# A half tile of the contraction as two 64-row matmuls on two PSUM banks, with one pool of three PSUM tiles for the product and the transform

## The chip, the cores and the metric

One Trainium2 chip, one of its cores. The metric is the device time of one execution in microseconds (us). TensorE (PE) multiplies matrices from SBUF into PSUM, loading one operand as weights (PEld) and streaming the other; ScalarE (ACT), VectorE (DVE) and GpSimd (POOL) do the elementwise work; SyncE (SP), ACT and POOL issue DMAs.

## The reference

The input `A_q` (2048 x 448) is normalised over its last axis, and three things are added: the input, a gated long convolution (A), and a two-layer perceptron with Mish (B).

```
def _A_ref(q, k, v, shift_k, ssm_k, ssm_D):          # S = 2048, D = 448
    k_shift = sum of 4 taps of k along S, each times shift_k[:, tap]
    kv = k_shift * v
    y = irfft(rfft(kv, 2 S) * rfft(ssm_k, 2 S))[:S] + kv * ssm_D
    return q * y
def _B_ref(x, w1, b1, w2):                           # F = 1792
    h = x @ w1 + b1
    act = h * tanh(softplus(h))                      # Mish
    return act @ w2
x = A_q
xn = _layernorm(x)
return x + _A_ref(xn, A_k, A_v, A_shift_k, A_ssm_k, A_ssm_D) + _B_ref(xn, B_w1, B_b1, B_w2)
```

## The kernel before

**The perceptron.** The 2048 rows go in 8 chunks of 256 (`CH`), the 1792 inner features in 14 tiles of 128, taken in pairs: 8 x 7 = 56 pairs (chunk c, pair p). Operands are float32, and the matmuls take a faster form that is rounded, so each operand is split into a rounded high part and the rest: `w1h` and `w1l`, `XH` and `XL`. A product is then high x high, low x high and high x low.

The contraction of the first product has 448 rows: three tiles of 128 and a half tile of 64. The half tile is packed: the input carries its 64 weight rows twice, and `tail` repeats the last 64 columns of the normalised x, so that tile 3 of x has the same 64 rows in both halves. `w1_lo` (L341) replaces rows 64 to 127 of tile 3 of `w1h` by the low part of the weights. One full matmul with tile 3 thus gives high plus low weights in one go.

`g1_mm` (L433) does one pair: for each of two inner tiles n, into its half of one PSUM bank, 3 high-high, 3 high-low and 3 low-high matmuls, and two with tile 3, one for `XH` (`th`) and one for `XL` (`tl`): 22 matmuls of 128 x 128 by 256 columns. `mish` (L449) reads the bank with two activations on ACT, then splits the result (`split`, L72: a copy on ACT and a subtraction on DVE). `g2_mm` (L461) multiplies by w2, two pairs later (`G2_LAG`).

**The transform.** The long convolution is done as matrix products in float32 with small tiles of the array (32 or 64 rows by 32 or 64 columns), in bursts: `f1_mm` (L117, two PSUM tiles, read by `f1_fold` on ACT and DVE), `f2_mm` (L201, one tile each, copied out by ACT), `i1_mm` (L243, two tiles, copied out by ACT) and `i2_mm` (L300, one tile, read by `gate` on DVE). Between the stages the data goes through DRAM.

**The x tiles.** For the next chunk, `ln_T` (L420) transposes the normalised x on TensorE into a PSUM tile, once in the odd slot of the last pair but one and once in the even slot of the last pair; ACT makes `XH` of it (L418) and DVE `XL` (L416).

**PSUM.** It has 8 banks. `g1p` holds two tiles of one bank, for `g1_mm` and `ln_T` in turn; `g2p` two of one bank, for `g2_mm`; `pcp` two of two banks, for the bursts. A pool hands out its tiles in turn, and the first write to a tile waits until what was in it has been read.

**The order** is written out by hand. Each pair has two slots. `mlp_slot` does `g1_mm(i)` in the even one, and in the odd one `mish(i)` and `g2_mm(i - 2)`. `plan` holds work to be put ahead of a slot's perceptron part and `plan2` work behind it; the dictionaries at the top and the loops from L519 on fill them. Each engine takes its instructions in this order. `drip` is a list of small DVE steps (the statistics of the next chunk), which `dv` lets in between others, and which `ln_T` empties.

Of the kernel before, what the change touches and what calls it, by code (L numbers as in the profile page):

```python
# [7 lines left out]
F32 = mybir.dt.float32  # L8
# [3 lines left out]
PSUM = bass.MemoryType.PSUM  # L12
# [6 lines left out]
CH = 256  # L19
# [18 lines left out]
def tile_kernel(ctx: ExitStack, tc, q, k, v, sk, hT, sD, w1, b1, w2, c_f1, c_g, c_gi, c_i2, out):  # L38
    nc = tc.nc
    V = nc.vector  # L40

    def pool(name, bufs=1, stack=ctx, **kw):
        return stack.enter_context(tc.tile_pool(name=name, bufs=bufs, **kw))
# [1 line left out]
    cp = pool("consts")  # L45
    wp = pool("weights")
    mp = pool("mlp")
    g1p = pool("ps_g1", 2, space=PSUM)
    g2p = pool("ps_g2", 2, space=PSUM)
    pcp = pool("ps_c", 2, space=PSUM)  # L50
    dp = pool("scratch", space=DRAM)


# [13 lines left out]
    w1h = wp.tile([128, 4, F], F32R, name="w1h")  # L67
# [4 lines left out]
    def split(h, l, raw):  # L72
        nc.scalar.copy(h, raw)  # L73
        V.tensor_sub(l, raw, h)  # L74

    def pc():
        return pcp.tile([128, 2, 512], F32, name="pc")
# [4 lines left out]
    def dv(n=1):  # L82
        for _ in range(n):
            if drip:
                drip.pop(0)()
# [246 lines left out]
    RW = {}  # L332
# [8 lines left out]
    def w1_lo(p, a=0, b=256, engs=(V, V)):  # L341
        fs, rw = slice(256 * p + a, 256 * p + b), RW["1", p][:, :, a:b]
        if engs[0]:
            engs[0].tensor_sub(w1l[:, :, fs], rw[:, 0:3], w1h[:, 0:3, fs])
        if engs[1]:
            engs[1].tensor_sub(w1h[64:128, 3, fs], rw[64:128, 3], w1h[64:128, 3, fs])

    def w1_split(p):
        w1_hi(p)
        w1_lo(p)  # L350
# [11 lines left out]
    def ln_load(c, eng=None):  # L362
        Q[c] = mp.tile([128, 2, D], F32, name="qt", tag="qt", bufs=3)
        if c:
            nc.sync.dma_start(Q[c], q[:, 2 * c:2 * c + 2])
        else:
            for jj in range(2):
                nc.sync.dma_start(Q[c][:, jj], q[:, jj])
# [30 lines left out]
    def ln_stats(c):  # L399
        stats, aggr, eps, power, norm, tail = ln_parts(c)  # L400
        drip.extend([lambda: stats(0), lambda: stats(1), lambda: aggr(0), lambda: aggr(1), lambda: eps(0, 2),
                     lambda: [f(*a) for f, *a in ((power, 0, 2), (norm, 0), (norm, 1), (tail, 0, 2))]])

    def transposes(c, jj, p):
        for kt in range(4):
            nc.tensor.transpose(p[:, 128 * kt:128 * kt + 128], XN[c][:, jj, 128 * kt:128 * kt + 128], ident)  # L406

    def x_tiles(c):
        XS[c] = (mp.tile([128, 4, CH], F32R, name="XH", tag="XH", bufs=2),
                 mp.tile([128, 4, CH], F32R, name="XL", tag="XL", bufs=2))  # L410

    def x_split(c, jj, p, lo):
        x = p.rearrange("p (a b) -> p a b", a=4)
        h, l = (t[:, :, 128 * jj:128 * jj + 128] for t in XS[c])
        if lo:
            V.tensor_sub(l, x, h)  # L416
        else:
            nc.scalar.copy(h, x)  # L418

    def ln_T(c, jj):  # L420
        if jj == 0:
            dv(len(drip))
            x_tiles(c)
        p = g1p.tile([128, 2, CH], F32, name="pg1").rearrange("p a b -> p (a b)")
        transposes(c, jj, p)
        for lo in range(2):
            x_split(c, jj, p, lo)
# [5 lines left out]
    def g1_mm(i):  # L433
        c, p = pairs[i]
        XH, XL = XS[c]
        ps = g1p.tile([128, 2, CH], F32, name="pg1")
        for n in range(2):
            f = 2 * p + n
            fs = slice(128 * f, 128 * f + 128)
            mm = []  # L440
            hh, hl, lh = ([(w[:, kt, fs], x[:, kt]) for kt in range(3)] for w, x in ((w1h, XH), (w1h, XL), (w1l, XH)))
            th, tl = ((w1h[:, 3, fs], x[:, 3]) for x in (XH, XL))

            mm = hh + hl + lh + [th, tl] if i == 0 and n else hh + lh + [th] + hl + [tl]
            for n_, (l, r) in enumerate(mm):
                nc.tensor.matmul(ps[:, n], l, r, start=n_ == 0, stop=n_ == len(mm) - 1)  # L446
        P1[i] = ps

    def mish(i):  # L449
        p = pairs[i][1]  # L450
        ps = P1.pop(i)
        a = mp.tile([128, 2, CH], F32, name="a", bufs=2)
        for n in range(2):
            nc.scalar.activation(a[:, n], ps[:, n], AF.Mish, bias=b1t[:, 2 * p + n:2 * p + n + 1])  # L454
        ah = mp.tile([128, 2, CH], F32R, name="ach", bufs=3)
        al = mp.tile([128, 2, CH], F32R, name="acl", bufs=3)
        split(ah, al, a)
        dv()
        AHL[i] = ah, al

    def g2_mm(i, jjs=(0, 1)):  # L461
        c, p = pairs[i]
        ah, al = AHL[i]
        for n in range(2):
            f = 2 * p + n
            for jj in jjs:
                if f == 0:
                    P2[c, jj] = g2p.tile([128, 512], F32, name="pg2")
                ps = P2[c, jj][:, :D]
                cs = slice(128 * jj, 128 * jj + 128)  # L470
                nc.tensor.matmul(ps, ah[:, n, cs], w2h[:, f], start=f == 0, stop=False)  # L471
                nc.tensor.matmul(ps, ah[:, n, cs], w2l[:, f], start=False, stop=False)  # L472
                nc.tensor.matmul(ps, al[:, n, cs], w2h[:, f], start=False, stop=f == NF - 1)  # L473

    def g2_evac(c, jjs=(0, 1)):
        x = Q[c]
        for jj in jjs:
            V.tensor_add(x[:, jj], P2.pop((c, jj))[:, :D], x[:, jj])  # L478
            dv()
            if late(c):  # L480
                nc.sync.dma_start(out[:, 2 * c + jj], x[:, jj])
        if not late(c):
            nc.sync.dma_start(out[:, 2 * c:2 * c + 2], x)

    def mlp_slot(s):
        i, half = divmod(s, 2)
        n = len(pairs)
        j = i - G2_LAG
        if half == 0:
            if i < n:  # L490
                c, p = pairs[i]
                if c + 1 < NCHUNK:
                    if p == 0:
                        ln_load(c + 1)
                    if p == (2 if c else 3):
                        ln_stats(c + 1)
                    if c == 0:
                        dv(len(drip))
                    if p == NP - 1:
                        ln_T(c + 1, 1)  # L500
                g1_mm(i)
        else:
            if i < n:
                c, p = pairs[i]
                if p == NP - 2 and c + 1 < NCHUNK:
                    ln_T(c + 1, 0)
                mish(i)
            if 0 <= j < n - 1:
                g2_mm(j)
            elif j == n - 1:  # L510
                for jj in range(2):
                    g2_mm(j, (jj,))
                    g2_evac(pairs[j][0], (jj,))
# [94 lines left out]
    ps = [g2p.tile([128, 512], F32, name="pg2") for _ in range(2)]  # L608
    x_tiles(0)
    for jj in range(2):  # L610
        norm(jj)
        tail(jj, jj + 1)
        transposes(0, jj, ps[jj])
        x_split(0, jj, ps[jj], 0)
    w1_lo(0, 0, 128)
    w1_hi(0, 128, 256)
    w1_lo(0, 128, 256, (nc.gpsimd, None))
    for jj in range(2):
        x_split(0, jj, ps[jj], 1)
# [3 lines left out]
    for s in range(nslots):  # L623
        j = s // 2 - G2_LAG - 1
        if s % 2 == 0 and j >= 0 and pairs[j][1] == NP - 1:
            g2_evac(pairs[j][0])
        for fn, args in plan.pop(s, ()):
            fn(*args)
        mlp_slot(s)
        for fn, args in plan2.pop(s, ()):  # L630
            fn(*args)
# [63 lines left out]
```

## Time and profile before

| | |
|---|---|
| median of 3 runs | 375.84 us (372.77 to 376.81) |
| profiled execution, first to last instruction (its span) | 370.5 us; its whole time is not among the numbers |
| PE busy | 361.2 us, 98%, 3128 matmul instructions |
| PEld (weight loads) busy | 292.2 us, 79% |
| DVE, ACT, POOL busy | 261.4 us (71%), 165.9 us (45%), 71.2 us (19%) |
| mean granted clock of TensorE | 1.000 |

The profile follows one execution. A row of the timeline reads: start, length, engine, line of the kernel, operation, tile written <- tiles read, rows * columns of the array, shapes, count; in brackets the engine's idle time before it and what ended it. Rows with a count are several instructions in one. Matmuls overlap in the records, so their spacing, and not their length, tells what one costs. A row of the groups reads: busy us, mean ns of one | idle time before.

### The profile page before, as it was taken

What the parts mean: (1) busy time and instruction counts of PE and PEld (TensorE: products, weight loads), DVE (VectorE), ACT (ScalarE), POOL (GpSimd) and SP (SyncE); (2) the same over time, 40 slices, a digit from 0 to 9 for tenths busy, and PEclk for the clock granted to TensorE, in tenths of its full rate; (3) what the DMA queues carried; (4) which work ended last, traced back from release to release, by engine and by line L of the source; (5) the groups of instructions that cost most, each with busy time, mean ns of one, the idle gap of its engine ahead of it and who ended that gap; (6) DMA issues with size and microseconds to landing.
All of it is one profiled execution on the core that took longest, in us unless ns stands there. A gap on an engine that the chain in (4) does not pass through costs nothing.

```text
span 370.5 us, 7467 instructions
## 1 busy us (share of the span) xinstructions
PE 361.2 (98%) x3128; PEld 292.2 (79%) x3128; DVE 261.4 (71%) x358; ACT 165.9 (45%) x277; POOL 71.2 (19%) x59
## 2 busy tenths in 40 slices
PE   8999999999998999999999999999999999999995
PEld 2889888888887988988886666666666879889885
DVE  4899748999968987996435647654474842997751
ACT  2785642343423333343353556555475533235450
POOL 2107002722070223520014000060000005102020
PEclk9999999999999999999999999999999999999999
DMA  8999968757596428504876498988494475949655
GB/s 307 319 308 355 382 233 233 215 159 239 145 294 184 104 58 262 179 25 99 264 235 216 135 282 239 272 271 237 134 328 110 105 239 207 407 195 293 102 69 129
DMA packets 31442, 79.35 MB, mean 214 GB/s; under 512 B 2865, under 2 KB 18098, under 8 KB 31410
## 3 DMA queue, kind: packets, MB, share of 16 engines
q1 hardware_dynamic: 19826, 44.35, 35.4%
q10 hardware_dynamic: 9248, 22.61, 23.0%
q0 software_dynamic: 2336, 11.93, 11.3%
q8 instruction: 24, 0.39, 0.4%
q14 instruction: 8, 0.07, 0.0%
HBM read 50.44 MB, written 28.44 MB: 213 GB/s over the span
## 4 chain that ended last, share of the span: by engine, by line
PE 62%; DVE 4%; ACT 2%; ACTq 1%; issue 1%; DVEq 0%
PE pg L446 24%; PE pg L471 8%; PE pg L473 8%; PE pg L472 8%; PE pc L207 7%; PE pc L250 3%; PE pc L307 2%; PE pc L124 1%; PE pg L406 1%; ACTq L261 1%; ACT a L454 1%; DVE x L171 1%; DVE yc L240 1%; DVE qt L478 0%; ACT XH L418 0%
## 5 line engine op out<-in xcount | busy, mean ns | idle before, releaser
L454 ACT ACTIVATE a<-pg,b1t 128x256 f32<-128x256 f32 x112 | 47.1, 472 | 101.4 <-PE pg L446 80.6
L446 PE MATMUL pg<-XH,w1h 128*128 128x256 f32 x448 | 91.2, 285 | 0.7 <-ACT XH L418 0.7
L446 PEld LDWEIGHTS pg<-XH,w1h 128*128 128x128 f32 x448 | 69.5, 188 | 18.1 <-issue 15.7
L471 PE MATMUL pg<-w2h,ach 128*128 128x448 f32 x224 | 83.0, 371 | 0.0
L472 PE MATMUL pg<-w2l,ach 128*128 128x448 f32 x224 | 81.4, 363 | 0.6 <-DVE w2l L74 0.6
L473 PE MATMUL pg<-w2h,acl 128*128 128x448 f32 x224 | 81.4, 363 | 0.0
L74 DVE TENSOR_TENSOR acl<-a,ach 128x512 fp32r<-128x512 f32 x56 | 38.8, 692 | 55.2 <-ACT ach L73 55.0
L446 PE MATMUL pg<-XL,w1h 128*128 128x256 f32 x448 | 69.6, 277 | 0.0
L446 PEld LDWEIGHTS pg<-XL,w1h 128*128 128x128 f32 x448 | 59.4, 188 | 0.1
L446 PE MATMUL pg<-XH,w1l 128*128 128x256 f32 x336 | 56.9, 278 | 0.0
L471 PEld LDWEIGHTS pg<-w2h,ach 128*128 128x128 f32 x224 | 42.0, 187 | 11.6 <-issue 9.4
L446 PEld LDWEIGHTS pg<-XH,w1l 128*128 128x128 f32 x336 | 46.8, 188 | 0.1
L472 PEld LDWEIGHTS pg<-w2l,ach 128*128 128x128 f32 x224 | 42.1, 188 | 3.5 <-DVE w2l L74 1.1
L473 PEld LDWEIGHTS pg<-w2h,acl 128*128 128x128 f32 x224 | 42.1, 188 | 2.5
L387 POOL TENSOR_TENSOR rstd<-ve,mhalf 128x2 f32<-128x2 f32 (+1 forms) x9 | 8.5, 945 | 162.6 <-DVE ve L384 105.8
L73 ACT CAST ach<-a 128x512 fp32r<-128x512 f32 x56 | 34.7, 620 | 1.8
L154 POOL TENSOR_TENSOR x<-kr,skb 128x896 f32<-128x896 f32 x8 | 17.0, 2129 | 74.9 <-DVE x L153 54.1
L171 DVE TENSOR_TENSOR x<-x 128x896 f32<-128x896 f32 x24 | 26.6, 1107 | 5.1 <-POOL x L154 4.4
L391 POOL TENSOR_SCALAR xn<-qt,mv,rstd 128x448 f32<-128x448 f32 x12 | 26.7, 2231 | 0.6
L418 ACT CAST XH<-pg 128x512 fp32r<-128x512 f32 x16 | 9.4, 587 | 38.7 <-PE pg L406 35.5
L416 DVE TENSOR_TENSOR XL<-pg,XH 128x512 fp32r<-128x512 f32 x16 | 10.9, 687 | 15.5 <-ACT XH L418 15.3
L130 ACT COPY st<-pc 128x896 f32<-128x896 f32 x16 | 14.5, 908 | 14.7 <-PE pc L124 12.8
(71 smaller groups left out, 401.1 us busy)
## 6 DMA issues: line engine op xcount, KB each, us to landing
Dh<-st ACTq DMA_DIRECT2D x16, 448.0 KB, 6.0
Dkv<-st ACTq DMA_DIRECT2D x16, 448.0 KB, 5.1
ah<-Dh SPq DMA_DIRECT2D x8, 896.0 KB, 6.8
av<-Dkv SPq DMA_DIRECT2D x8, 896.0 KB, 5.9
E<-qe ACTq DMA_DIRECT2D x16, 448.0 KB, 5.4
e<-E POOLq DMA_DIRECT2D x8, 896.0 KB, 7.7
kr<-in_k_dram SPq DMA_DIRECT2D x10, 448.0 KB, 6.2
kr<-in_w_dram SPq DMA_DIRECT2D x7, 512.0 KB, 6.3
```

The costliest lines, as they stand in the source:

```text
L73: nc.scalar.copy(h, raw)
L74: V.tensor_sub(l, raw, h)
L130: nc.scalar.copy(st[:, 1], o)
L154: nc.gpsimd.tensor_mul(o, KR[g - u // 2], skb[:, u:u + 1].to_broadcast([128, 2, D]))
L171: V.tensor_add(KV[g], KV[g], o)
L207: nc.tensor.matmul(p[32 * t:32 * t + 32, r, :D], g[rs, t, c], a[rs, t], start=True, stop=True, tile_position=(64 * r, 32 * t))
L391: eng.tensor_scalar(xn[:, jj, :D], Q[c][:, jj], mv[:, j, 0:1], rstd[:, j:j + 1], op0=ALU.subtract, op1=ALU.mult)
L446: nc.tensor.matmul(ps[:, n], l, r, start=n_ == 0, stop=n_ == len(mm) - 1)
L454: nc.scalar.activation(a[:, n], ps[:, n], AF.Mish, bias=b1t[:, 2 * p + n:2 * p + n + 1])
L471: nc.tensor.matmul(ps, ah[:, n, cs], w2h[:, f], start=f == 0, stop=False)
L472: nc.tensor.matmul(ps, ah[:, n, cs], w2l[:, f], start=False, stop=False)
L473: nc.tensor.matmul(ps, al[:, n, cs], w2h[:, f], start=False, stop=f == NF - 1)
```

## The change

Four edits belong together.

1. In `g1_mm`, the matmul with tile 3 and `XL` goes for both inner tiles. In its place stand, at the end of the pair, two matmuls of 64 rows: the first with rows 0 to 63 for inner tile 0, the second with rows 64 to 127 for inner tile 1, each with high weights and low x. The product of low weights and low x, which the full matmul gave as well, is not made any more for these 64 rows.
2. So that the second finds high weights in rows 64 to 127, `w1_lo` puts the low part of the odd inner tiles into rows 0 to 63; it is now one subtraction for each 128 columns.
3. The two matmuls write to two banks, so `g1_mm` takes a tile of two banks. `g1p` is gone; the pool `pcp` has three tiles, in turn for `g1_mm`, `ln_T` and the transform's bursts.
4. In the odd slot of the last pair but one, `mish(i)` comes ahead of `ln_T(c + 1, 0)`.

```
-    g1p = pool("ps_g1", 2, space=PSUM)
     g2p = pool("ps_g2", 2, space=PSUM)
-    pcp = pool("ps_c", 2, space=PSUM)
+    pcp = pool("ps_c", 3, space=PSUM)
...
         if engs[1]:
-            engs[1].tensor_sub(w1h[64:128, 3, fs], rw[64:128, 3], w1h[64:128, 3, fs])
+            for n in range(a // 128, b // 128):
+                rs, fs = slice(64 - 64 * n, 128 - 64 * n), slice(256 * p + 128 * n, 256 * p + 128 * n + 128)
+                engs[1].tensor_sub(w1h[rs, 3, fs], RW["1", p][rs, 3, 128 * n:128 * n + 128], w1h[rs, 3, fs])
...
-        p = g1p.tile([128, 2, CH], F32, name="pg1").rearrange("p a b -> p (a b)")
+        p = pc()[:, 0]
...
-        ps = g1p.tile([128, 2, CH], F32, name="pg1")
+        ps = pc()[:, :, :CH]
...
-            th, tl = ((w1h[:, 3, fs], x[:, 3]) for x in (XH, XL))
-
-            mm = hh + hl + lh + [th, tl] if i == 0 and n else hh + lh + [th] + hl + [tl]
+            th = w1h[:, 3, fs], XH[:, 3]
+            mm = hh + hl + lh + [th] if i == 0 and n else hh + lh + [th] + hl
             for n_, (l, r) in enumerate(mm):
-                nc.tensor.matmul(ps[:, n], l, r, start=n_ == 0, stop=n_ == len(mm) - 1)
+                nc.tensor.matmul(ps[:, n], l, r, start=n_ == 0, stop=False)
+        for n in range(2):
+            rs, f = slice(64 * n, 64 * n + 64), 2 * p + n
+            nc.tensor.matmul(ps[:, n], w1h[rs, 3, 128 * f:128 * f + 128], XL[rs, 3], start=False, stop=True, tile_position=(64 * n, 0))
...
+                mish(i)
                 if p == NP - 2 and c + 1 < NCHUNK:
                     ln_T(c + 1, 0)
-                mish(i)
```

## The prediction

> **What bounds the kernel now.** I read the page first (busy times, chain), then the groups by line and shape, then TensorE's timeline stage by stage, then for each PSUM tile its first write against its last read.
>
> ```profile
> span 370.5 us, 7467 instructions
> PE 361.2 (98%) x3128; PEld 292.2 (79%) x3128; DVE 261.4 (71%) x358; ACT 165.9 (45%) x277; POOL 71.2 (19%) x59
> PE 62%; DVE 4%; ACT 2%; ACTq 1%; issue 1%; DVEq 0%
> ...
> L446 PE MATMUL pg<-XL,w1h 128*128 128x256 f32 x448 | 69.6, 277 | 0.0
> ...
> 137.66 2.51 PE pg L446 x22
> ```
>
> TensorE is busy 98% of the span and is most of the chain, so every microsecond added to its in-order stream, or that it waits, lengthens the run nearly one for one. The first product of one pair is 22 matmuls in 2.51 us (last row, from the chain), 0.114 us each. The two x-low half tiles are 2 of the 8 XL matmuls a pair (448 / 56).
>
> **The pair of half tiles.** The change removes two full matmuls, 2 x 0.114 = 0.23 us a pair, and adds two 64-row ones that could run side by side. No row shows 64 rows x 128 columns. The nearest are the transform's bursts, which also leave the full array for a row tiling:
>
> ```profile
> 102.58 0.23 PEld L124 LDWEIGHTS pc<-x,f1id 32*64 32x64 f32 x16 [0.31 <-issue]
> ...
> 183.24 0.62 PE L446 MATMUL pg<-XL,w1h 128*128 128x256 f32 x4
> 183.79 1.73 PE L207 MATMUL pc<-ah,g 64*32 64x448 f32 x32
> ...
> 184.19 1.33 PE L207 MATMUL pc<-ah,g 64*32 64x448 f32 x24
> ...
> 184.56 0.96 PE L207 MATMUL pc<-ah,g 64*32 64x448 f32 x16
> 185.45 0.47 PE L471 MATMUL pg<-w2h,ach 128*128 128x448 f32 x1
> 185.76 0.36 PE L472 MATMUL pg<-w2l,ach 128*128 128x448 f32 x1
> 185.97 0.37 PE L473 MATMUL pg<-w2h,acl 128*128 128x448 f32 x1
> ```
>
> Tiles do run side by side: 32 instructions go in four rounds of eight, and a round costs 0.37 (184.19 to 184.56). But each visit has a price outside its streams. Going in: four full matmuls from 183.24 should end at 183.24 + 4 x 0.114 = 183.70, yet the burst starts at 183.79: 0.09. Coming out: the last two rounds start at 184.56 and the next full matmul at 185.45, so 0.89 less 2 x 0.37 is 0.15; about 0.05 of it is that eight tiles start one behind another (sixteen loads begin within about 0.1 in the first row), which leaves 0.10. Then the first full matmul cannot hide its weight load: 185.45 to 185.76 is 0.31 where the next step is 0.21, so 0.10. The pair's own first load, also 128 columns wide, is exposed likewise: 0.10. With the stream of 0.11 that is 0.09 + 0.10 + 0.11 + 0.10 + 0.10 = 0.50 against 0.23: **+0.27 us**. Counting along the timeline, in 17 of the 56 pairs TensorE does a burst right after the product, and there the way in and out is paid already in part: without the pair 0.23 + 0.09, with it 0.09 + 0.10 + 0.11 + 0.10 = 0.40, **+0.08**. Sum: 39 x 0.27 + 17 x 0.08 = **+11.9 us**. Bounds: no price for the switch and full overlap, 56 x (-0.11) = -6.4; loads and streams of the two halves one after the other, 0.2 more a pair, +23. I take the middle because entering and leaving cost the same wherever a burst stands.
>
> The Trainium skill speaks for less: TensorE: Matmul & The Clock Gate, Part 3 (The mechanism), says a weight load is pulled ahead of matmuls in flight when it goes to another row group. By that the loads would hide, and the second rival below would hold. The first row here has a load that waited for the burst before it could begin.
>
> **The shared PSUM tiles.** Before, the product rotates over two tiles of its own and the transform over two. After, every product, transform and x transpose takes the next of three, in program order, so each one needs the third one before it to be read out. I set the start of each on TensorE against the last read of the third before it. Most have microseconds to spare. These do not:
>
> ```profile
> 39.24 1.01 PE L124 MATMUL pc<-x,f1id 32*64 32x448 f32 x16
> 40.18 0.66 PE L406 MATMUL pg<-f1id,xn 128*128 128x128 f32 x4
> 40.59 0.60 PE L446 MATMUL pg<-XH,w1h 128*128 128x256 f32 x3
> 40.87 0.59 ACT L418 CAST XH<-pg 128x512 fp32r<-128x512 f32 x1 [1.12 <-PE pg L406]
> 41.35 0.92 ACT L130 COPY st<-pc 128x896 f32<-128x896 f32 x1
> 42.30 1.09 DVE L131 TENSOR_TENSOR st<-pc,st 128x896 f32<-128x896 f32 x1
> 43.43 1.09 DVE L133 TENSOR_TENSOR st<-pc,st 128x896 f32<-128x896 f32 x1
> ```
>
> Here the burst takes two tiles, the transpose the third, and the product at 40.59 needs the burst's first, which L133 reads until 44.52. The four readers in between depend on each other and none is late, so TensorE stands still for **3.9 us**. The same order of work returns at 79, and two others resemble it:
>
> ```profile
> 12.67 0.50 PE L446 MATMUL pg<-XH,w1h 128*128 128x256 f32 x3
> 14.23 1.09 DVE L133 TENSOR_TENSOR st<-pc,st 128x896 f32<-128x896 f32 x1
> ...
> 79.97 0.66 PE L406 MATMUL pg<-f1id,xn 128*128 128x128 f32 x4
> 80.39 0.60 PE L446 MATMUL pg<-XH,w1h 128*128 128x256 f32 x3
> 83.93 1.08 DVE L131 TENSOR_TENSOR st<-pc,st 128x896 f32<-128x896 f32 x1
> 85.04 1.09 DVE L133 TENSOR_TENSOR st<-pc,st 128x896 f32<-128x896 f32 x1
> ...
> 121.05 0.60 PE L406 MATMUL pg<-f1id,xn 128*128 128x128 f32 x4
> 123.10 1.09 DVE L133 TENSOR_TENSOR st<-pc,st 128x896 f32<-128x896 f32 x1
> ```
>
> At 80.39 the wait would be 5.7, but part is VectorE's backlog, which TensorE's extra time shortens: between 3.9 and 5.7, I take **4.6** (with a 1.5 us wait of the transposes just before, from the same backlog). At 121.05: 3.1 to the end of L133, less the added TensorE time that it hides, **2.0**. At 12.67: 2.6; it hides about 0.6 of waits for weights that TensorE has later, and the next burst's fold then comes 0.8 late: **2.2** with the rest near it.
>
> ```profile
> 199.84 0.59 ACT L418 CAST XH<-pg 128x512 fp32r<-128x512 f32 x1 [5.97 <-PE pg L406]
> 200.32 0.84 ACT L454 ACTIVATE a<-pg,b1t 128x256 f32<-128x256 f32 x2
> 201.72 1.70 ACT L218 COPY hs<-pc 128x896 f32<-128x896 f32 x2
> 202.68 1.79 PE L207 MATMUL pc<-av,g 64*32 64x448 f32 x32 [0.46 <-ACT hs L218]
> 204.81 0.60 PE L446 MATMUL pg<-XH,w1h 128*128 128x256 f32 x3
> 205.57 1.73 ACT L227 COPY vs<-pc 128x896 f32<-128x896 f32 x2
> ...
> 264.70 1.79 PE L207 MATMUL pc<-ah,g 64*32 64x448 f32 x32 [0.47 <-ACT qe L258]
> 268.43 0.58 ACT L418 CAST XH<-pg 128x512 fp32r<-128x512 f32 x1 [2.98 <-issue]
> ```
>
> **Mish ahead of the transposes.** ScalarE now waits 6 us for the transposes although the product is ready; moved ahead, L454 frees its tile before the transposes ask for it (three conflicts of 2.0 each vanish, here, at 118 and at 261), and L218 comes a microsecond or more sooner, so the 0.46 wait at 202.68 goes. What the move puts back: the XH cast, XL and, on VectorE, the activation's low part now goes before XL and whatever statistics were still due; the transposed x is needed a product or more later, so I cost that at nothing. But the product at 204.81 needs the tile that L227 copies from 205.57 to 206.45: 1.6 - 0.5 = **1.1**. The like place after 264.70 has up to 3.0, most of it the 2.98 that ScalarE spends issuing stores, which begins earlier once the copies ahead of it do; I take 1.4 less the 0.8 of TensorE's waits that vanish there, **0.6**.
>
> Sum of the waits: 3.9 + 4.6 + 2.0 + 2.2 + 1.1 + 0.6 = **+14.4 us**. Bounds: all conflicts at face value without the three that vanish, 25; none, if the tiles are not handed out in strict turn, 0.
>
> **The weights' low half.** One subtraction of a 64-row x 256 block becomes two of 128 columns:
>
> ```profile
> L346 DVE TENSOR_TENSOR w1h<-kr,w1h 64x256 fp32r<-64x256 f32 x6 | 2.9, 476 | 0.2
> L346 DVE TENSOR_TENSOR w1h<-kr,w1h 64x128 fp32r<-64x128 f32 x2 | 1.1, 540 | 0.1
> ```
>
> Six more instructions, at most 2 x 540 - 476 = 0.6 each. All sit in the first 40 us on VectorE and one lies ahead of the fold at 12.67: +0.1 to +0.6 there. VectorE's remaining waits are TensorE's, so I take **+0.3**.
>
> **Forecast.** 11.9 + 14.4 + 0.3 = +26.6. The profiled execution spans 370.5, and what lies around it is not told; the three runs have a median of 375.84, 5.3 above the span. I add the sum to that median: 402.4, **402 us**.
>
> **Rivals.** (1) *The waits hide.* Only the pair's price is paid: 375.8 + 11.9 = 388. For it: the tiles freed by mish; against: the place at 40, where no reader is late. (2) *No switch price.* The half tiles cost 0.11 a pair, not 0.50, the loads hidden as the skill's rule would have it: 375.8 - 6.4 + 14.7 = 384. Against: every burst in the timeline pays going in and out. (3) *Faster.* A half-row tile of full width keeps the array's mode, so that 2 x 0.114 become 0.114 in every pair: 375.8 - 6.4 = 369.4 where the tiles are free in time. The place is the step from the last full matmul to the half one, which stays near 0.114; it decides as long as the waits for tiles stay under 6.4 in all. For it: a burst's tiles do share their streams; against it: the price of every burst's way in, and the 3.9 at 40 alone is over half of what it may lose. (4) *Dearer.* The two halves' loads and streams go one after the other (+11 more), or the conflicts come near face value (+10): 412 to 413. (5) *The clock falls in the stalls.*
>
> ```profile
> 368.00:370.40 2.40, 0.00 (x0) 0.00 (x0) 0.00 (x0) 0.00 (x0) 0.00 (x0) 1.00 0.25 96
> 370.00:372.00 2.00, 0.00 (x0) 0.00 (x0) 0.00 (x0) 0.00 (x0) 0.00 (x0) 0.82 0.00 0
> ```
>
> After the last matmul (record ends at 366.6) the granted clock was still 1.00 until 370.40 and fell only then, so some 4 us of idleness are safe and the stall at 80 is near the edge. If it halves for one 2.51 us product after two stalls, that is +5: 407. The Trainium skill, TensorE: Matmul & The Clock Gate, Part 1 (What's actually happening), lets the clock halve after one idle window of about 3.4 us; by that both long stalls would do it.
>
> **How the numbers follow.** Forecast 0.52; waits hide 0.15; no switch price 0.10; faster 0.06; dearer 0.12; clock 0.05. The range 384 to 416 takes in rivals 1, 2, 4 and 5 and leaves out rival 3 and the far ends of the bounds. A measurement here tells about 1% from no change (3.8 us). Faster by more than that: rival 3, 0.06. Within it: 0.03, the near edge of rivals 1 and 2 where both hold in part. Slower: 0.91.
>
> **What would show it.** Right: the L446 group has 20 full matmuls a pair plus two 64*128 ones whose starts lie within 0.02 of each other; the step into them is about 0.2 where it was 0.114, and the next full matmul starts 0.3 after them; TensorE waits for DVE L133 near 41 and 83 for about 4 us each; its busy time per pair is about the same, its idle time up by 14. Wrong: steps of 0.114 into and out of the half tiles; no wait of TensorE for L133 over 1 us; or a span under 385.

## The result, and the profile after

In the first comparison the changed kernel took 390.46 us (median of 4, 389.17 to 396.12) and the kernel before 375.98 (4 runs, 372.77 to 376.81): ratio 1.0451 [1.0403, 1.0500]. Two later comparisons, with 17 and 11 runs of the kernel before (medians 372.41 and 372.38), gave 392.11 and 391.55: 1.0521 [1.0485, 1.0558] and 1.0496 [1.0463, 1.0529]. One of the four runs of the changed kernel, the profiled one of 396.12, had a lower granted clock (0.987), and the ratios leave such runs out, so that they need not be the quotients of the medians. So the change costs 4.5 to 5.2%, by the medians some 14 to 20 us. The forecast had the sign and the price of the pair of half tiles; it had the waits for tiles wrong, and was about 10 to 12 us too high.

What follows is a later profile of the same kernel. That execution took 391.74 with a span of 390.0, so 1.7 us lie around the span, in both kernels alike (371.94 and 370.2 in a run of the kernel before). Spans are compared with spans: 390.0 - 370.5 = +19.5.

From the page of the changed kernel and its groups by line: span, busy times, the product's costliest group and the new group of half tiles.

```profile
span 390.0 us, 7477 instructions
PE 376.1 (96%) x3128; PEld 294.9 (76%) x3128; DVE 262.5 (67%) x364; ACT 166.3 (43%) x277; POOL 70.6 (18%) x59
...
L446 PE MATMUL pc<-XH,w1h 128*128 128x256 f32 x448 | 92.6, 288 | 8.4 <-DVE XL L417 6.7
...
L449 PE MATMUL pc<-XL,w1h 64*128 64x256 f32 x112 | 21.5, 380 | 0.0
```

TensorE has as many matmuls as before, 3128, but is busy 14.9 us longer and idle 4.6 us longer (13.9 against 9.3). VectorE and ScalarE do nearly the same work (VectorE has the six added subtractions). And there is a row that before had nothing like it: 8.4 us of idleness ahead of the product, 6.7 of it ended by `XL` (L417), not by the transform's fold.

TensorE's timeline of the changed kernel, the end of one product and what follows; then another, with a burst behind it.

```profile
138.94 0.50 PE L446 MATMUL pc<-XL,w1h 128*128 128x256 f32 x3
139.37 0.38 PE L449 MATMUL pc<-XL,w1h 64*128 64x256 f32 x2
139.69 0.47 PE L474 MATMUL pg<-w2h,ach 128*128 128x448 f32 x1
139.99 0.37 PE L475 MATMUL pg<-w2l,ach 128*128 128x448 f32 x1
```

```profile
14.93 0.52 PE L446 MATMUL pc<-XL,w1h 128*128 128x256 f32 x3
15.37 0.19 PEld L449 LDWEIGHTS pc<-XL,w1h 64*128 64x128 f32 x2
15.37 0.38 PE L449 MATMUL pc<-XL,w1h 64*128 64x256 f32 x2
...
15.69 1.01 PE L123 MATMUL pc<-x,f1id 32*64 32x448 f32 x16
```

The third full matmul starts at 138.94 + 2 x 0.114 = 139.17; the halves follow 0.206 later (0.114 between full matmuls). The second half starts 3 ns after the first, and the two weight loads likewise: they do run side by side. The next full matmul starts 0.313 after the first half, 0.310 after the second, and its own next step is 0.306 where 0.20 is normal. With two full matmuls in their place the three steps would be 0.114 each and the fourth 0.20: the pair costs 0.206 + 0.313 + 0.106 - 3 x 0.114 = +0.283 us. In the second timeline a burst starts 0.313 after the first half; with full matmuls it would be 2 x 0.114 + 0.203 from the last, so +0.085. Over the kernel: 39 x 0.283 + 17 x 0.085 = 12.5 us. (Four of the 39 stand ahead of transposes and cost some 0.1 less.)

Waits of TensorE, changed kernel (engine, line waited for: total, times, longest), then those of the kernel before that it no longer has.

```profile
PE pc L446 <- DVE XL L417: 6.7, 4, 2.5
...
PE pc L446 <- ACT a L457: 0.8, 1, 0.8
PE pc L446 <- ACT XH L419: 0.7, 1, 0.7
...
PE pc L446 <- DVE x L152: 0.2, 1, 0.2
```

```profile
PE pc L124 <- DVE x L174: 1.1, 1, 1.1
...
PE pc L207 <- ACT hs L218: 0.8, 2, 0.5
...
PE pg L472 <- DVE w2l L74: 0.6, 1, 0.6
PE pc L207 <- ACT qe L258: 0.5, 1, 0.5
PE pc L250 <- DVE yc L240: 0.4, 1, 0.4
```

Taken as steps over the normal one, so with the weight loads that stand behind a wait, the waits within the stream are 9.3 us after and 4.0 before: +5.3. The four waits for `XL` are at 43, 88, 219 and 283. Here is the first, from the timeline of all engines.

```profile
40.12 1.01 PE L123 MATMUL pc<-x,f1id 32*64 32x448 f32 x16
...
41.06 0.66 PE L407 MATMUL pc<-f1id,xn 128*128 128x128 f32 x4
...
42.37 0.69 DVE L417 TENSOR_TENSOR XL<-pc,XH 128x512 fp32r<-128x512 f32 x1 [1.19 <-ACT XH L419]
...
43.12 0.62 PE L446 MATMUL pc<-XH,w1h 128*128 128x256 f32 x3 [1.40 <-DVE XL L417]
43.18 1.09 DVE L130 TENSOR_TENSOR st<-pc,st 128x896 f32<-128x896 f32 x1
...
44.31 1.09 DVE L132 TENSOR_TENSOR st<-pc,st 128x896 f32<-128x896 f32 x1
```

The product starts 0.06 after `XL` ends (43.06) and 2.3 **before** the fold has read the burst's tiles (L132 ends at 45.40). It therefore doesn't write the burst's first tile, the one that strict turn would give it; it took the transposes' own. So the pool, unlike what is said of it ahead of the prediction, does not hand out its tiles in strict turn. That the next one taken is the one whose reads come first in the order of the program, here the transposes', is a reading of the traces and was not tried by itself.

The second wait, with TensorE's clock in windows (busy time of each engine, then granted clock, DMA share, GB/s). Here L129 had read out the burst's second tile by 86.80, 1.1 us before the product started, and the product still waited for `XL` (87.85): the order of the program decides, not which tile is free first in time.

```profile
83.78 1.01 PE L123 MATMUL pc<-x,f1id 32*64 32x448 f32 x16
...
85.89 0.91 ACT L129 COPY st<-pc 128x896 f32<-128x896 f32 x1
...
87.17 0.68 DVE L417 TENSOR_TENSOR XL<-pc,XH 128x512 fp32r<-128x512 f32 x1
...
87.91 1.01 PE L446 MATMUL pc<-XH,w1h 128*128 128x256 f32 x3 [2.54 <-DVE XL L417]
...
88.71 0.84 PE L446 MATMUL pc<-XH,w1l 128*128 128x256 f32 x3
```

```profile
88.00:91.40 3.40, 3.40 (x17) 3.40 (x18) 1.94 (x2) 0.00 (x0) 0.00 (x0) 0.53 0.84 281
91.40:94.00 2.60, 2.60 (x17) 2.23 (x16) 0.12 (x1) 1.46 (x3) 0.00 (x0) 1.00 0.00 0
```

After 2.5 us of standing still the clock is halved for 3.4 us: the product's matmuls come 0.21 apart. That costs 3.4 / 2 = 1.7 us. The three together, 12.5 + 5.3 + 1.7 = 19.5, account for the 19.5 by which the spans differ. (Setting the two executions side by side, matmul by matmul, gives about 12.2, 5.6 and 1.7.)

### The profile page after: what moved, and what is told of

Its sections match the earlier page's. It is cut to its first block, busy times and chain, and to the rows that moved or that the text cites. A ratio compares the mean times of both kernels' runs of the same rounds, so it can differ in the third digit from the quotient of the medians.

```text
span 394.3 us, 7477 instructions
## 1 busy us (share of the span) xinstructions
PE 377.9 (96%) x3128; PEld 296.5 (75%) x3128; DVE 262.8 (67%) x364; ACT 166.4 (42%) x277; POOL 70.4 (18%) x59
## 4 chain that ended last, share of the span: by engine, by line
PE 61%; DVE 5%; issue 1%; ACT 1%; DVEq 0%
PE pc L446 21%; PE pg L474 9%; PE pg L476 7%; PE pg L475 7%; PE pc L206 7%; PE pc L249 3%; PE pc L449 3%; PE pc L306 2%; PE pc L407 1%; PE pc L123 1%; DVE acl L73 1%; DVE x L170 1%; DVE XL L417 1%; DVE yc L239 1%; DVE qt L481 0%
## 5 line engine op out<-in xcount | busy, mean ns | idle before, releaser
L457 ACT ACTIVATE a<-pc,b1t 128x256 f32<-128x256 f32 x112 | 47.1, 471 | 141.5 <-PE pc L449 132.5
L446 PE MATMUL pc<-XH,w1h 128*128 128x256 f32 x448 | 92.6, 289 | 8.6 <-DVE XL L417 6.8
L446 PEld LDWEIGHTS pc<-XH,w1h 128*128 128x128 f32 x448 | 70.5, 191 | 27.3 <-issue 14.3
L474 PE MATMUL pg<-w2h,ach 128*128 128x448 f32 x224 | 87.2, 389 | 0.0
L446 PE MATMUL pc<-XH,w1l 128*128 128x256 f32 x336 | 57.8, 281 | 0.0
L446 PE MATMUL pc<-XL,w1h 128*128 128x256 f32 x336 | 57.4, 280 | 0.0
L446 PEld LDWEIGHTS pc<-XH,w1l 128*128 128x128 f32 x336 | 47.8, 191 | 0.0
L446 PEld LDWEIGHTS pc<-XL,w1h 128*128 128x128 f32 x336 | 47.4, 191 | 0.0
L153 POOL TENSOR_TENSOR x<-kr,skb 128x896 f32<-128x896 f32 x8 | 17.0, 2124 | 88.0 <-DVE x L152 65.0
L170 DVE TENSOR_TENSOR x<-x 128x896 f32<-128x896 f32 x24 | 26.6, 1106 | 4.9 <-POOL x L153 4.3
L449 PE MATMUL pc<-XL,w1h 64*128 64x256 f32 x112 | 21.6, 383 | 0.0
L129 ACT COPY st<-pc 128x896 f32<-128x896 f32 x16 | 14.5, 908 | 16.3 <-PE pc L123 16.3
L130 DVE TENSOR_TENSOR st<-pc,st 128x896 f32<-128x896 f32 x16 | 17.4, 1087 | 4.6 <-ACT st L129 2.9
```

The lines of the kernel that those rows point to most:

```text
L130: V.tensor_add(st[:, 0], e, st[:, 1])
L170: V.tensor_add(KV[g], KV[g], o)
L446: nc.tensor.matmul(ps[:, n], l, r, start=n_ == 0, stop=False)
L449: nc.tensor.matmul(ps[:, n], w1h[rs, 3, 128 * f:128 * f + 128], XL[rs, 3], start=False, stop=True, tile_position=(64 * n, 0))
```

## The experiments

They ran in three groups. Where a diff doesn't say otherwise, it starts from the changed kernel. The first four ran beside the kernel before at 372.73 us, the next ones at 372.41; the last one, and the second repeat of the changed kernel, at 372.38.

**Full matmuls in place of the halves.** All of the sharing and the order stays.

```
-            rs, f = slice(64 * n, 64 * n + 64), 2 * p + n
-            nc.tensor.matmul(ps[:, n], w1h[rs, 3, ...], XL[rs, 3], ..., tile_position=(64 * n, 0))
+            f = 2 * p + n
+            nc.tensor.matmul(ps[:, n], w1h[:, 3, 128 * f:128 * f + 128], XL[:, 3], start=False, stop=True)
```

> The changed kernel with its three shared PSUM tiles, its order and its weight layout, but the two 64-row matmuls of each pair replaced by two full 128-row matmuls with tile 3 and x low, as before the change. Theory (going to 64-row tiles and back costs 0.28 us a pair, 0.08 where a burst follows, 12.5 us in all; the waits for tiles are the rest): 378 us, 12.5 below the changed kernel's 390.5 and about 2 above the kernel before. Rival (the waits for shared tiles carry the loss): it stays at 388 to 390, since all sharing is still there.

Measured: 381.2 us, 1.0222 [1.0184, 1.0261]; span 378.8. That is 3 us above the 378 expected, and far from the rival's 388. The full matmuls take back half to three fifths of the loss (a ratio lower by 0.023 to 0.030, 8.5 to 11 us); the sharing of tiles, with the order and the layout of the weights that belong to it, costs the other 8.5 us (381.2 less 372.73). Its waits:

```profile
PE pc L446 <- DVE XL L417: 7.5, 4, 3.3
PE pc L446 <- ACT a L457: 1.2, 1, 1.2
```

They are longer than with the halves (11.3 against 9.3 in all): TensorE comes earlier to the same places, and VectorE does not. So the pair had hidden some of the waits, and taking it away gives back 11.2 between the spans (390.0 less 378.8) and not 12.5.

**One visit for each half.** Each half stands behind its own inner tile's full matmuls: two changes of the tiling a pair, and no streams side by side.

```
         for n in range(2):
...
-        for n in range(2):
-            rs, f = slice(64 * n, 64 * n + 64), 2 * p + n
-            nc.tensor.matmul(ps[:, n], w1h[rs, 3, ...], XL[rs, 3], ...)
+            rs = slice(64 * n, 64 * n + 64)
+            nc.tensor.matmul(ps[:, n], w1h[rs, 3, fs], XL[rs, 3], start=False, stop=True, tile_position=(64 * n, 0))
```

> The changed kernel with each 64-row matmul right behind the 20-matmul pair's own half it belongs to (inner tile 0's after its ten, inner tile 1's after its ten), so that the array goes into 64-row tiles twice a pair. Theory (a visit costs 0.51 us with its stream, whatever it does): 56 more visits between full matmuls, +28.6 us, 419 us. Rival (the price lies in the two streams and loads running one after the other inside a visit, not in going in and out): the same two streams and loads, so within 3 us of 390.5.

Measured: 419.69, 1.1258 [1.1220, 1.1296]; span 417.9, 27.9 over the changed kernel, as the price of a visit says. The streams themselves, 0.11 each, cannot make 56 more of them cost 28 us; that rival falls. In this kernel the clock fell twice: at 93.4, behind a wait of 2.3 us that ended at 92.9, and at 236.7, shown here in timeline and windows.

```profile
231.11 1.73 PE L206 MATMUL pc<-av,g 64*32 64x448 f32 x32
232.78 0.66 PE L407 MATMUL pc<-f1id,xn 128*128 128x128 f32 x4
234.83 0.62 PE L446 MATMUL pc<-XH,w1h 128*128 128x256 f32 x3 [1.40 <-DVE XL L417]
```

```profile
233.00:236.70 3.70, 2.30 (x16) 1.81 (x15) 0.94 (x2) 2.21 (x3) 0.00 (x0) 1.00 0.70 207
236.70:240.10 3.40, 3.40 (x26) 2.48 (x33) 0.00 (x0) 0.74 (x2) 0.00 (x0) 0.50 0.23 83
240.10:243.00 2.90, 2.90 (x40) 1.88 (x25) 2.12 (x3) 2.25 (x4) 0.00 (x0) 0.99 0.02 6
```

Only a wait of 1.40 us stands ahead of this fall, which came nearly 2 us after its end and lasted 3.4. The same wait at the like place of the changed kernel (219.51) left the clock alone.

**No halves at all.** The product of the high weights and the low x of the last 64 rows is left out.

```
-        for n in range(2):
-            rs, f = ...
-            nc.tensor.matmul(ps[:, n], w1h[rs, 3, ...], XL[rs, 3], ...)
+                nc.tensor.matmul(ps[:, n], l, r, start=n_ == 0, stop=n_ == len(mm) - 1)
```

> The changed kernel without the two 64-row matmuls (the product of high weights and low x for the last 64 rows of the contraction is left out). Theory (a visit of 0.51 us, 0.31 where a burst follows): 39 x 0.51 + 17 x 0.31 = 25 us below the changed kernel, 365 us, and 56 x 0.228 = 12.8 us below the kernel with full matmuls in their place. Rival (the halves cost about one full matmul, 0.114, and the waits do the rest): 56 x 0.114 = 6.4 below, 384.

Measured: 373.17, 1.0024 [1.0003, 1.0044]; span 372.2. A miss by 8 against the 365 expected: 112 full matmuls fewer than in the first experiment, 12.8 us of stream, brought 8.0. TensorE's timeline and the windows of this kernel:

```profile
83.46 1.01 PE L446 MATMUL pc<-XH,w1h 128*128 128x256 f32 x3 [3.27 <-DVE XL L417]
```

```profile
84.00:88.00 4.00, 4.00 (x21) 4.00 (x20) 1.49 (x2) 0.00 (x0) 0.00 (x0) 0.50 0.60 242
88.00:91.40 3.40, 3.40 (x17) 3.13 (x17) 1.75 (x3) 1.46 (x3) 0.00 (x0) 0.80 0.33 69
```

Its waits add up to 14.9 us, 3.6 more than in the first experiment, and the half clock lasts longer (mean clock 0.986 against 0.995, some 3.3 us): the faster stream runs ahead of VectorE, stands still longer, and pays again in the clock. 12.8 - 3.6 - 3.3 = 5.9, against 6.6 between the spans. The ten runs of this kernel say what the lower clock does to the time: the five with a mean clock of 0.986 took 373.53 to 374.71 us, the five with 0.995 took 372.23 to 372.81. Between their medians lie 1.3 us, so less than half of the 3.3 comes out as time; what makes up for the rest is not shown.

**Transposes ahead of the burst.** `ln_T(c + 1, 1)` is issued before the burst of its slot, so that its tile is read out while the burst runs.

```
-                    if p == NP - 1:
-                        ln_T(c + 1, 1)
...
+        if p_ == NP - 1 and c_ + 1 < NCHUNK:
+            ln_T(c_ + 1, 1)
         for fn, args in plan.pop(s, ()):
```

> The changed kernel with the second x transposes of a chunk moved ahead of the burst of the same slot, so that XH and XL of it are made while the burst runs. Theory on the waits (a product can only take a tile that is given back in program order, and behind burst and transposes that is the transposes' one, free after XL; four such waits of 1.6, 2.8, 1.6 and 1.6 us): they shrink by the burst's 0.9 or 1.7, about 5 us less, 385.5. Rival (the tile comes in strict turn, so the product waits for the burst's first tile and its two DVE folds): no gain, 390 to 391.

Measured: 389.63 (388.05 to 394.75), 1.0436 [1.0388, 1.0484]; span 386.3. The waits fell from 9.3 to 5.5, 3.8 where 5 was expected, and the span by 3.7. The ratio fell less, and its interval overlaps two of the changed kernel's three, so a gain in time is likely but not shown. The rival doesn't follow as recorded: with the transposes ahead of the burst, the third tile before the product is theirs in strict turn too, so this experiment does not tell the two rules apart; the two timelines above do. At the worst place the wait stays (2.69 on TensorE), in the timeline:

```profile
81.89 0.60 PE L407 MATMUL pc<-f1id,xn 128*128 128x128 f32 x4
...
85.38 0.69 DVE L417 TENSOR_TENSOR XL<-pc,XH 128x512 fp32r<-128x512 f32 x1
...
86.12 0.71 PEld L446 LDWEIGHTS pc<-XH,w1h 128*128 128x128 f32 x3 [3.46 <-DVE XL L417]
```

`XL` comes 2.9 us after its transposes: VectorE is late there, whatever the order on TensorE.

**The changed kernel again**, in the second and the third group.

> The changed kernel once more, beside the variants that are to be compared with it. Theory (pair of half tiles about 12 us, waits for shared tiles 5 us net, part of it at a lower clock): 4 to 5% above the kernel before. Rival (the earlier ratio belonged to that chip): within 2% of the kernel before.

> The changed kernel on the same chip as the one with idle work in its waits: 4.5 to 5.2% above the kernel before, clock 0.993 to 0.998, by either account.

Measured: 392.11 and 391.55, as told above.

**Halves beside a burst.** In the 23 pairs whose product follows a burst the halves go first; elsewhere last. They touch a burst in 32 pairs instead of 17.

```
+FIRST = (2, 4, 8, 10, 12, 16, 17, 22, 25, 30, 35, 36, 37, 38, 39, 40, 42, 43, 45, 49, 51, 53, 55)
...
+        if i in FIRST:
+            halves(True, False)
         for n in range(2):
...
+        if i not in FIRST:
+            halves(False, True)
```

> The changed kernel with the two 64-row matmuls put first in those 23 pairs that follow a burst, and left last in the other 33. A visit then stands beside a burst in 32 pairs and not in 17. Theory (beside a burst one way in or out is paid already, 0.20 us less): 15 x 0.20 = 3.0 us below the changed kernel. Rival (the price is in the loads and streams of the halves themselves, wherever they stand): no difference from the changed kernel within 1 us.

Measured: 388.86, 1.0432 [1.0391, 1.0473], which is 3.25 us less than the changed kernel beside it. 15 pairs moved to a burst's edge save 15 x 0.2 = 3.0. TensorE's timeline of this kernel shows the way out paid once for both:

```profile
140.69 1.01 PE L124 MATMUL pc<-x,f1id 32*64 32x448 f32 x16
141.63 0.38 PE L442 MATMUL pc<-XL,w1h 64*128 64x256 f32 x2
141.94 0.62 PE L454 MATMUL pc<-XH,w1h 128*128 128x256 f32 x3
```

From the burst's last matmul to the halves it is 0.46, as from a burst to a full matmul, so the way in costs nothing more here. The price is therefore that of entering and leaving the tiling, not of the halves.

**Full matmuls and transposes ahead of the burst**: the edits of the first and the fourth experiment together.

> Full matmuls in place of the halves, shared tiles, mish ahead, and the second transposes ahead of the burst. Theory (four waits of 1.6 to 3.3 us for the transposes' tile shrink by the burst that now runs meanwhile): 3.5 to 5 us below the kernel with full matmuls that waits (2.2% above the kernel before), so about 1% above the kernel before. Rival (the waits only move to the next tile): as without the move, 2.2% above.

Measured: 382.18, 1.0252 [1.0210, 1.0293]; no gain over the first experiment (1.0222 [1.0184, 1.0261]). The 1% that was expected is missed, and the rival holds: the waits are 9.9 instead of 11.3, but one of 2.2 us moved to 273, and the clock halved there. The wait of 2.9 us that is left at 84.1 did not halve it.

**Only the order of mish.** The kernel before, with `mish(i)` ahead of `ln_T(c + 1, 0)`.

```
+                mish(i)
                 if p == NP - 2 and c + 1 < NCHUNK:
                     ln_T(c + 1, 0)
-                mish(i)
```

> The kernel before with its own pools and full matmuls; only mish goes ahead of the first transposes of a chunk. Theory (ScalarE waits some 6 us for the transposes there, so the copies behind come 1 to 2 us sooner and TensorE's waits of 0.5, 0.5 and 0.4 us at 203, 265 and 270 go): 1.4 us below the kernel before, 0.4%. Rival (XH and XL come later by the same and the product of the next chunk waits for them): not faster, 0 to +2 us.

Measured: 371.96 (12 runs), 0.9979 [0.9960, 0.9997]; span 369.9. This is the fastest complete version found, but only by 0.2% (0.4% was expected), with an interval that barely leaves out no change. Its waits:

```profile
PE pg L446 <- DVE x L153: 0.5, 1, 0.5
...
PE pg L446 <- DVE XL L416: 0.3, 1, 0.3
```

The waits for `hs` and `qe` (1.3 us) are gone, as the prediction had it; two new ones (0.8) took their place, which the prediction costed at nothing. Both are for `XL`: the first row names `x`, a fill of one element (L153), which ends within 2 ns of an `XL`.

**Filling the waits.** Matmuls with a zero operand go into an open sum of the second product ahead of the four products that wait; they change no value.

```
+FILL = {6: 7, 13: 12, 34: 7, 41: 7}
...
+        for _ in range(FILL.get(i, 0)):
+            nc.tensor.matmul(P2[c, 0][:, :D], w1h[:, 0, 0:128], zero[:, 0:1].to_broadcast([128, D]), start=False, stop=False)
         ps = pc()[:, :, :CH]
```

> The changed kernel with idle work in TensorE's four longest waits: ahead of the products of pairs 6, 13, 34 and 41, 7, 12, 7 and 7 full matmuls of 448 columns with a zero operand, which add nothing to the second product's open sum (0.2 us each, less than each wait of 1.6, 2.8, 1.6 and 1.6). Theory (the granted clock halves for 3.4 us or more because TensorE stood idle in those waits): the clock is 1.000, and the time 1.7 us or more below the changed kernel beside it. Rival (the lower clock has another cause, the sequence of tile shapes for one): the clock stays at 0.993 to 0.998 and the time is the same or up to 1 us longer.

Measured: 393.01 (391.24 to 394.87), 1.0552 [1.0517, 1.0586], beside 1.0496 [1.0463, 1.0529] for the changed kernel: not faster. In the profiled run the mechanism is there (timeline, then windows):

```profile
86.24 2.55 PE L439 MATMUL pg<-zero,w1h 128*128 128x448 f32 x12
...
89.02 0.63 PE L449 MATMUL pc<-XH,w1h 128*128 128x256 f32 x3 [0.23 <-DVE XL L418]
```

```profile
88.00:91.40 3.40, 3.17 (x25) 2.79 (x23) 3.05 (x4) 0.00 (x0) 0.00 (x0) 1.00 0.91 315
```

The clock stays at 1.00 and the product's matmuls come 0.114 apart. Beside the profile of the changed kernel of the same group (span 391.2, against 389.5 here), matmul by matmul, 1.7 us of half clock are all that differs in sum. But the medians do not follow, and three of its six runs had mean clocks of 0.987 to 0.994. In the same group the changed kernel took 389.34 and 389.52 in its two runs at 0.998 and 0.999, and 391.48 to 392.95 in the four at 0.991 to 0.994, so the lower clock goes with some 2 us more there; the filled kernel at 0.998 to 1.000 took 391.24 to 392.38. Both profiles of this group also have a wait at the start, for the load of `x` (1.9 us here, 2.5 in the changed kernel), which the profile of the changed kernel shown above has not. Such a wait may be what hides the gain in the median; this was not tried.

## Why the prediction was right, and where it was off

**The pair of half tiles** was forecast at +11.9, 0.27 and 0.08 a pair; the trace has 0.283 and 0.085, 12.5 in all, and three experiments agree (full matmuls, once its longer waits are counted, one visit for each half, and halves beside a burst). Its parts were right too, as far as they can be told apart: 0.09 in (0.206 less 0.114), the halves' load and stream and the way out together (0.310), and 0.10 for the next load. Rivals 2 and 3 fall with the step into the halves, 0.206; the Trainium skill, TensorEngine Tiling (Array Packing), Key Properties, has a change of the tiling mode drain TensorE, and the trace agrees, with 0.09 us on the way in; the way out cannot be told apart within the 0.310. The bound of loads and streams one after the other falls with the 3 ns.

**The waits for tiles** are the term that was mis-sized: forecast +14.4, measured 9.3 over normal steps, while 4.0 of the kernel before are gone: +5.3. What failed is the sentence that each use takes the next of three and so needs the third before it. I had kept that as a bound of 0 "if the tiles are not handed out in strict turn", and they are not. One of the signs of being wrong that the prediction lists came true: no wait of TensorE is for L133 (now L132). Behind a burst with transposes the product waits for `XL`, not for the fold:

| place before | forecast | measured | what ends it |
|---|---|---|---|
| 12.67 | 2.2 | 0.8, one product later | the activation L457 |
| 40 | 3.9 | 1.6 | `XL` |
| 80 | 4.6 | 2.8 | `XL` |
| 121 | 2.0 | about 0.6 | mostly `XL` (the view names L152, which ends with it) |
| 204 | 1.1 | 1.6 | `XL` |
| 266 | 0.6 | 1.6 | `XL` |

The last two were put too low, and for another reason. At 204 the forecast named the first copy of L227 (now L226) as what the product waits for, and took 0.5 off because TensorE's own wait ahead of the burst goes. The timeline of the changed kernel there:

```profile
215.78 1.73 PE L206 MATMUL pc<-av,g 64*32 64x448 f32 x32
...
218.62 1.72 ACT L226 COPY vs<-pc 128x896 f32<-128x896 f32 x2
218.76 0.69 DVE L417 TENSOR_TENSOR XL<-pc,XH 128x512 fp32r<-128x512 f32 x1 [0.85 <-ACT XH L419]
...
219.51 0.62 PE L446 MATMUL pc<-XH,w1h 128*128 128x256 f32 x3 [1.40 <-DVE XL L417]
```

The product starts when `XL` has ended (219.45). The first of the two copies ends 0.03 after that start, at 219.54, so waiting for its tile would have taken as long. What failed is the deduction: the copies begin 2.84 after the burst (218.62 less 215.78), 2.89 before the change, because transposes, `XH` and copies all follow the burst. When the burst starts earlier they start earlier too, and so does the product, and the wait stays whole. At 266 the first copy ends 0.03 after the product's start likewise, and the 0.8 taken off there fails in the same way. So five of the six places were found, the tile that each one waits for was wrong, and it made the forecast too dear behind the bursts that VectorE reads.

Rival 1 (the waits hide, 388) came nearer in number, but its reason is not the one: 9.3 us of waits are there, and 4.0 older ones went.

**Mish ahead of the transposes** was right that the waits near 202 and 264 go, and wrong that what it puts back costs nothing (0.8 in the experiment with that edit alone). Undoing this edit alone in the changed kernel wasn't tried: by the order of the program, bursts and product would hold all three tiles there, and the transposes would have none.

**The clock.** Rival 5 said some 4 us of idleness are safe, read from the end of the run. It isn't so: the clock halved around a wait of 2.54 us. The rival's effect exists, but with one window and 1.7 us, not two and 5.

**The base.** I added the sum to the median shown, 375.84. What lies around a span is about 1.7, not 5.3; two of the three runs shown were simply high, and the 17 and 11 runs of the later comparisons have medians of 372.4. From the profiled execution the same sum gives 370.5 + 1.7 + 26.6 = 398.8. Against the later medians (392) the forecast of 402.4 has a surplus of 10.4, made up to within 0.1 by these terms: 9.1 are the waits (14.4 - 5.3), 3.4 the base (375.84 - 372.4) and 0.3 the weights, whose additions show nowhere by themselves; the pair (0.6) and the clock (1.7) go the other way.

## What to carry to other kernels

Price a change of TensorE's tiling by the visit and not by the matmul: here a visit with one matmul on each of two tiles costs 0.28 us more than two full matmuls, and still 0.08 more at the edge of a burst, so it pays in neither place. Each further matmul on each tile would save 0.11 by the overlap. By these numbers, as an estimate that was not tried, it takes four on each tile between full matmuls, or two at a burst's edge, to come out ahead. Before working out waits for a shared pool, find which buffer a use really takes (start of the writer against the last read of each candidate); a rule for it that no trace shows is the first thing to doubt. And an engine that is 98% busy hides the waits of the others: work taken off it comes back in part as standing still.

## What the runs showed of the hardware that was not expected

TensorE's clock fell to half beside far shorter waits than the end of the run suggested:

| kernel | wait, us | ends at | half clock from | for, us |
|---|---|---|---|---|
| changed | 2.54 | 87.9 | 87.8 | 3.4 |
| without the halves | 3.27 | 83.5 | 82.5 | 6.8 |
| without the halves | 1.98 | 122.3 | 123.5 | 3.4 |
| one visit for each half | 1.40 | 234.8 | 236.7 | 3.4 |
| full matmuls, transposes ahead | 2.15 | 273.2 | 273.4 | 3.4 |
| changed | 1.40 | 219.5 | none | |
| full matmuls, transposes ahead | 2.92 | 84.1 | none | |

So the length of the wait alone does not decide. Each time the half clock lasted one or two stretches of 3.4 us. In the clock's records of one execution the changes also lie whole multiples of 3.413 us apart (in the changed kernel at 5.885, 87.805 and 91.218), so where a wait falls between them may matter. Right before most of these waits stands a burst of small tiles (with four short transposes before or behind it), so that TensorE did little for 3.7 to 4.1 us (231.11 to 234.83, 83.78 to 87.91); at 122.3 full matmuls stand right before the wait and the burst behind it. Whether a burst counts as idleness was not tried, and what decides stays open. The Trainium skill, TensorE: Matmul & The Clock Gate, Part 1 (What's actually happening), gives windows of about 3.4 us, halved after an idle one; the length of the half clock agrees, while the waits themselves were shorter than that, and nothing here shows whether the time beside them counts.
